# Retention and two gated layers on one core: a third raw and a third sum buffer in the rounds' dead input, weight combinations on GpSimd, 28 preparations beside the two rounds

## The chip, the core and the metric

The kernel runs on one core of one Trainium2 chip. The metric is the device time of one execution in microseconds (us); three executions of the kernel before gave 852.07, 852.21 and 853.77 us, and their median, 852.21 us, is the time before. A separately profiled execution supplies the trace; it took 853.28 us, of which the profile's span covers 851.6 us.

Engine names as in the profile: PE is TensorE (PEld its weight load), DVE is VectorE, ACT is ScalarE, POOL is GpSimd, SP is SyncE, whose queue issues nearly all transfers here.

## What is computed

```python
def reference(q, k, v, moe_w_in, moe_w_out, moe2_w_in, moe2_w_out):
    # q, k, v: (4, 8, 576, 64); scores are masked and decayed per head
    scores = q @ k.T / 8 * where(i >= j, gamma[h] ** (i - j), 0)
    x = (scores @ v) as (2304, 512)
    h = x @ moe_w_in                         # (512, 2048)
    x = (h * tanh(softplus(h))) @ moe_w_out  # (2048, 512)
    h = x @ moe2_w_in
    return (h * sigmoid(1.702 * h)) @ moe2_w_out
```

All numbers are float32. The kernel splits every float32 operand of the two layers into a high part and a low part (type float32r) and multiplies three of the four products of parts, so each block product is three matmuls.

## The kernel before

**The three stretches.** `attention` computes x into the tile `X`, which holds all 2304 tokens, 4 x 128 channels deep. `first_layer` then does the first layer's tokens 0 to 767 directly: for each of 16 weight blocks and two token blocks (512 and 256 wide) a slot with `up` (line 392) and `down` (line 413). Tokens 768 to 1535 and 1536 to 2303 follow in two *rounds*, which use the seven-product form of a 2 x 2 block product (Strassen-Winograd) for the up-projection (line 1105) and plain products for the down-projection (line 1042). `second_layer` does the second layer in three rounds of 768 tokens, seven products in both halves (up at line 648, down at line 697).

**The combined weights.** Seven products need sums of weight quarters (S1 to S4). For the first layer, `combine_first` makes them while the first layer runs, one call for each of 8 weight pairs: four additions of 128x256 by DVE (line 260), the high part by ACT, the low part by DVE (line 264), then transfers to a DRAM buffer `first_stream`, from which the rounds load them back into a ring of three buffers (line 986). For the second layer, 32 *preparations* (`prepare`, lines 275 to 337) do the same into the DRAM buffer `stream`. Before, 14 of them stand beside round one, 13 beside round two and 5 in the second layer's first round (`PREPARED_IN`).

**One preparation.** It loads raw weights (`cr`, 512 KB, line 283), clamps them on DVE (L191), converts their words on ACT (`rest`, `rebase`), sets the sign bits on DVE (L131, L203), joins the words on POOL (L207, two instructions) into the sum buffer `cy`, adds four combinations on DVE (L319 three times, L320), splits into a high part (ACT) and a low part (DVE, L328), and stores 896 KB into `stream` (line 331).

**What sets the order.** The whole program is in a fixed order per engine; nothing is rescheduled. A preparation is a generator: each `yield "skip"`, `"pool"`, `"act early"` or `"vector"` gives up control until the named position of the next table entry. A round passes 8 times over the 15 entries of `R_STEPS` (seven entries are a product of 6 matmuls, four are a down piece of 12, four do nothing on PE), so the number of yields fixes how many entries apart two steps of a preparation stand. A preparation begins every 6.5 entries (`EVERY`). `UNPREPARED` keeps preparations out of the last pass of each round. In the second layer's first round an entry is one up-product of 6 matmuls.

**What a preparation shares.** `live["cr"]` and `live["cy"]` admit two raw buffers and two sum buffers at a time. The order then has to satisfy the buffer's own waits: the join of preparation j + 2 writes the sum buffer that the store of preparation j still reads. Counted in entries from the start of preparation j, its join stands at 9, its additions at 12, its store at 20; the join of preparation j + 2 stands at 13 + 9 = 22 and its additions at 25.

**What the rounds put on the same engines.** A pass copies PSUM banks to the tile `c` on ACT (`pre`), adds a second bank on DVE (`plus`, L451 `c<-p,c`), applies the activation on ACT and makes the high part `g` (ACT) and the low part (DVE, L451 `g<-c,g`). Only two banks take products in a round (`A` and `E`), so PE may not begin a product in a bank until `pre` or `plus` has read what the bank held; between the two there is a down piece or a down piece and a product.

## Time and profile before

| What | Value |
|---|---|
| Time before, median of 3 runs | 852.21 us |
| Profiled execution, its own time | 853.28 us |
| Its span | 851.6 us |
| PE busy | 810.9 us (95%) |
| DVE busy | 597.8 us (70%) |
| ACT busy | 446.3 us (52%) |
| POOL busy | 105.9 us (12%) |
| Transfers | 219.67 MB, mean 258 GB/s |
| Chain that ended last | PE 69%, DMA 16%, DVE 6%, POOL 3%, issue 2%, ACT 2% |

PE's 95% is an average. Its share has to be read by stretch, because in most of the span PE has no gap at all and the missing time lies in a few places. Beside PE's share, the chain of waits tells what the span's end hung on: a share of DMA or POOL in it means that PE had run out of work that was ready. A busy row of POOL or DVE may also contain time in which the instruction was held up by the other engine.

### The profile page before, as it was taken

The page shows a single profiled execution, that of the slowest core. Times are in us where ns is not written, and L with a number is a line of the kernel's source. Part 1 is how long each engine was busy: PE and PEld are TensorE (multiplying, and loading weights), DVE is VectorE, ACT ScalarE, POOL GpSimd, SP SyncE. Part 2 cuts the span into 40 slices and gives each one's busy share as a digit, 9 for nine tenths or more (in the row PEclk, how much of TensorE's full clock was granted, in tenths as well). Part 3 has the DMA queues.
Part 4 walks back from the last instruction along what each step waited for, and adds up shares of the span by engine and source line. Part 5 has one row for each costly group of instructions (what it writes and reads, how often), then busy time and mean ns, then how long its engine had stood idle before and what let it go on. Part 6 is the DMA issues. An engine that isn't in the chain of part 4 may idle for free.

```text
span 851.6 us, 14187 instructions
## 1 busy us (share of the span) xinstructions
PE 810.9 (95%) x5392; PEld 764.8 (90%) x5392; DVE 597.8 (70%) x1118; ACT 446.3 (52%) x861; POOL 105.9 (12%) x124
## 2 busy tenths in 40 slices
PE   8999999999969979996989998999999999999998
PEld 7898888888969869996878997899999999999998
DVE  4886999997756657565655658688755689555776
ACT  5445777766645546554554554366333465233652
POOL 3452222220112120111111001000000000000000
PEclk9999999999979999998999999999999999999999
DMA  9974679746778785678876569987887778877775
GB/s 362 422 311 140 205 238 296 260 149 222 253 241 285 240 273 168 233 234 283 277 263 241 179 213 337 356 272 269 281 284 253 245 266 269 308 230 271 251 263 174
DMA packets 86132, 219.67 MB, mean 258 GB/s; under 512 B 5808, under 2 KB 51888, under 8 KB 78768
## 3 DMA queue, kind: packets, MB, share of 16 engines
q1 hardware_dynamic: 85920, 218.56, 75.3%
q8 instruction: 43, 0.70, 0.3%
q14 instruction: 25, 0.20, 0.1%
q10 hardware_dynamic: 144, 0.20, 0.1%
HBM read 169.98 MB, written 48.76 MB: 257 GB/s over the span
## 4 chain that ended last, share of the span: by engine, by line
PE 69%; DMA 16%; DVE 6%; POOL 3%; issue 2%; ACT 2%; SPq 0%; POOLq 0%; DVEq 0%
PE p L697 21%; PE p L648 17%; DMA stream<-cy 11%; PE h L392 8%; PE acc L413 7%; PE acc L1042 7%; PE p L1105 6%; POOL cy L207 2%; DMA unit<-qkv_dram 2%; DMA cr<-w_dram 1%; DVE cy L319 1%; PE o L901 1%; DMA raws<-w_dram 1%; PE sc L839 1%; DVE g L451 1%
## 5 line engine op out<-in xcount | busy, mean ns | idle before, releaser
L648 PE MATMUL p<-xop,ring 128*128 128x384 f32 x1008 | 176.6, 335 | 5.3 <-DVE cs L451 3.5
L648 PEld LDWEIGHTS p<-xop,ring 128*128 128x128 f32 x1008 | 174.5, 188 | 6.9 <-DVE cs L451 4.5
L697 PE MATMUL p<-g,ring 128*128 128x384 f32 x1008 | 175.2, 334 | 0.0
L697 PEld LDWEIGHTS p<-g,ring 128*128 128x128 f32 x1008 | 174.8, 188 | 0.0
L1105 PE MATMUL p<-xop,ring 128*128 128x384 f32 x672 | 132.8, 342 | 24.5 <-DVE c L451 22.5
L1042 PE MATMUL acc<-g,w 128*128 128x512 f32 (+1 forms) x768 | 147.8, 342 | 2.5 <-DVE g L451 2.5
L1042 PEld LDWEIGHTS acc<-g,w 128*128 128x128 f32 x768 | 126.8, 191 | 21.4 <-DVE g L451 4.1
L1105 PEld LDWEIGHTS p<-xop,ring 128*128 128x128 f32 x672 | 116.7, 190 | 28.3 <-DVE c L451 24.8
L122 ACT ACTIVATE g<-cs 128x384 fp32r<-128x384 f32 x168 | 79.0, 517 | 60.2 <-PE p L697 60.0
L451 DVE TENSOR_TENSOR g<-cs,g 128x384 fp32r<-128x384 f32 x168 | 90.0, 554 | 26.7 <-ACT g L122 25.1
L122 ACT ACTIVATE cs<-cs 128x384 f32<-128x384 f32 x72 | 37.7, 524 | 106.1 <-DVE cs L451 106.0
L413 PE MATMUL acc<-g,w 128*128 128x512 f32 (+1 forms) x384 | 72.3, 337 | 0.0
L413 PEld LDWEIGHTS acc<-g,w 128*128 128x128 f32 x384 | 60.2, 190 | 7.6
L207 POOL TENSOR_TENSOR cy<-cr 128x256 int32<-128x256 int32 x54 | 37.7, 718 | 231.7 <-DVE cr L203 83.0
L451 DVE TENSOR_TENSOR g<-c,g 128x384 fp32r<-128x384 f32 x64 | 37.2, 581 | 29.0 <-ACT g L122 28.4
L122 ACT ACTIVATE g<-c 128x384 fp32r<-128x384 f32 (+1 forms) x96 | 50.4, 525 | 12.4 <-PE acc L413 10.0
L122 ACT ACTIVATE cy<-cy 128x896 fp32r<-128x896 f32 (+1 forms) x40 | 38.8, 969 | 30.1 <-DVE cy L320 23.7
L451 DVE TENSOR_TENSOR cs<-cs 128x384 f32<-128x384 f32 x96 | 53.1, 553 | 0.8
L319 DVE TENSOR_TENSOR cy<-cy 128x128 f32<-128x128 f32 x96 | 25.1, 289 | 40.3 <-POOL cy L207 39.2
L207 POOL TENSOR_TENSOR raw<-raw 128x512 int32<-128x512 int32 x32 | 38.0, 1188 | 101.6 <-DVE raw L203 80.3
L122 ACT ACTIVATE raw<-raw 128x512 int32<-128x512 uint32 x64 | 41.8, 677 | 14.5 <-DVE raw L191 14.4
L122 ACT ACTIVATE c<-p 128x384 f32<-128x384 f32 x64 | 30.9, 484 | 34.7 <-PE p L1105 34.3
(90 smaller groups left out, 932.1 us busy)
## 6 DMA issues: line engine op xcount, KB each, us to landing
ring<-stream SPq DMA_DIRECT2D x112, 512.0 KB, 4.6
stream<-cy SPq DMA_DIRECT2D x32, 896.0 KB, 6.6
ring<-stream SPq DMA_DIRECT2D x28, 1024.0 KB, 4.8
raw<-w_dram SPq DMA_DIRECT2D x32, 512.0 KB, 7.5
unit<-qkv_dram SPq DMA_DIRECT2D x15, 1024.0 KB, 10.7
ring<-first_stream SPq DMA_DIRECT2D x14, 1024.0 KB, 7.2
ring<-first_stream SPq DMA_DIRECT2D x28, 512.0 KB, 5.9
cr<-w_dram SPq DMA_DIRECT2D x27, 512.0 KB, 4.3
```

Source lines behind the costliest of these rows:

```text
L122: nc.scalar.activation(out=o, in_=i, func=f, scale=scale, bias=bias)
L207: nc.gpsimd.tensor_tensor(out=o, in0=upper, in1=bits, op=ALU.add)
L319: nc.vector.tensor_tensor(out=v[:, o], in0=v[:, a], in1=v[:, b], op=op)
L392: nc.tensor.matmul(h[:, :n], lhsT=W[0, m // 2][:, m % 2, a, k * P : (k + 1) * P], rhs=xs[t, k][:, b, :n], start=((k, a, b) == order[0]), s ...
L413: nc.tensor.matmul(acc[t, e][:, :n], lhsT=W[1, m // 2][:, m % 2, a, e * P : (e + 1) * P], rhs=g[:, b, :n],  start=(begins(i) and a == 0 an ...
L451: eng.tensor_tensor(out=o, in0=a, in1=b, op=op)
L648: nc.tensor.matmul(banks[p], lhsT=w[:, k, a * P : (a + 1) * P], rhs=x[:, b, k], start=(p not in SAME and k == 0 and a == 0 and b == 0), st ...
L697: nc.tensor.matmul(banks[e, p], lhsT=w[:, e, a * P : (a + 1) * P], rhs=g[:, b], start=(p != 2 and r == 0 and a == 0 and b == 0), stop=(r = ...
L839: nc.tensor.matmul(sc[j][:n, p, :n], lhsT=kt[sl, p, :], rhs=qt[sl, p, :], start=True, stop=True)
L901: nc.tensor.matmul(o[sl, p, :n], lhsT=v[:n, p * P + 64 * j : p * P + 64 * j + 64], rhs=pm[u][j][:n, p, :n], start=(c == 0 and p == 0), sto ...
L1042: nc.tensor.matmul(acc[t, e][:, :w], lhsT=W[1, m // 2][:, m % 2, a, e * P : (e + 1) * P], rhs=g[:, b, o : o + w], start=(m == 0 and a == 0 ...
L1105: nc.tensor.matmul(bank, lhsT=w[:, a, k * P : (k + 1) * P], rhs=x[:, b, k], start=(p in (1, 2, 7) and k == 0 and a == 0 and b == 0), stop= ...
```

## The change

Five things are edited.

1. **Layout of X.** `X` was `[128, 4, 2304]`; it is now `[128, 3, 4, 768]`, so that the 768 tokens of one round are one contiguous stretch of 3072 elements in each partition. `cut` gives the old views; one store of `attention` that crosses a round's border becomes two. All other uses of `X` only change their indexing.
2. **A third raw buffer and a third sum buffer.** Once a round's input has been turned into operands, its part of `X` is dead until the round's results are written. `idle(s, o, n)` gives a piece of it. Every third preparation takes its raw weights and its sums from there; the four preparations of the second layer take three raw buffers and one sum buffer from the dead part of tokens 0 to 767, and the other sums from three further tiles. The limits on `live` go from 2 to 3.
3. **Combinations on GpSimd.** The four additions of `prepare` and the four of `combine_first` go from `nc.vector` to `nc.gpsimd`; in `prepare` they follow the two joins directly.
4. **Distances.** Clamp at entry 7 (4 before), sign at 10 (8), join and additions at 11 (9 and 12), high part at 15 (14), low part at 17 (17), store at 19 (20); the sum buffer is given back at 27 (21), the raw buffer at 14 (11).
5. **Counts.** `PREPARED_IN` goes from (14, 13, 5) to (14, 14, 4), and `UNPREPARED` is dropped: the positions are passed in the last pass of a round, too.

```diff
-UNPREPARED = (*range((NR - 1) * NE, NR * NE), *range((2 * NR - 1) * NE, 2 * NR * NE))
 EVERY = 6.5
-PREPARED_IN = (14, 13, 5)
+PREPARED_IN = (14, 14, 4)
...
-    X = keep.tile([P, NK, NT], F32, name="X")
+    X = keep.tile([P, NT // (2 * TH), NK, 2 * TH], F32, name="X")
...
+    def idle(s, o, n):
+
+        return X[:, s].rearrange("p k n -> p (k n)")[:, o : o + n]
...
         for o, a, b, op in ((s1, a21, a22, ALU.add), (s3, a11, a21, ALU.subtract), (s2, s1, a11, ALU.subtract), (s4, a12, s2, ALU.subtract)):
-            nc.vector.tensor_tensor(out=o, in0=a, in1=b, op=op)
+            nc.gpsimd.tensor_tensor(out=o, in0=a, in1=b, op=op)
+        yield "pool"
         yield "act early"
...
     def prepare(j, r, part, half):
 
-        while live["cr"] == 2:
+        late_one = j - sum(PREPARED_IN[:2])
+        s = 0 if late_one >= 0 else R_ROUNDS[j >= PREPARED_IN[0]]
+        while live["cr"] == 3:
             yield "skip"
         live["cr"] += 1
-        if j == sum(PREPARED_IN[:2]):
-            raws.append(keep.tile([P, 2, 4, P], I64, tag="side", name="raws"))
-        raw = raws[0][:, j % 2] if raws else keep.tile([P, 4, P], I64, tag=f"x{2 + j % 2}", name="cr")
-        nc.sync.dma_start(out=raw, in_=w2[r, part, half])
-        yield from pause(4)
+        if late_one >= 0:
+            raw = idle(0, late_one % 3 * 2 * DM, 2 * DM)
+        elif j % 3 == 2:
+            raw = idle(s, 4 * DM, 2 * DM)
+        else:
+            raw = keep.tile([P, 2 * DM], F32, tag=f"x{2 + j % 3}", name="cr")
+        raw = raw.rearrange("p (q n) -> p q n", q=4)
+        nc.sync.dma_start(out=raw.bitcast(I32), in_=w2[r, part, half].bitcast(I32))
+        yield from pause(7)
         yield "vector"
         clamp(raw)
-        yield "skip"
         yield "act early"
         rest(raw)
         yield "act early"
         rebase(raw, nc.scalar)
-        yield from pause(2)
+        yield "skip"
         yield "vector"
         sign(raw)
         yield "pool"
-        while live["cy"] == 2:
+        while live["cy"] == 3:
             yield "pool"
...
         join(raw[:, 0:2], bits[:, a11 : a21 + 1 : a21 - a11])
         join(raw[:, 2:4], bits[:, a12 : a22 + 1 : a22 - a12])
-        yield from pause(2)
+        for o, a, b, op in (
+            (s1, a21, a22, ALU.add),
+            (s3, a11, a21, ALU.subtract),
+            (s2, s1, a11, ALU.subtract),
+            (s4, a12, s2, ALU.subtract),
+        ):
+            nc.gpsimd.tensor_tensor(out=v[:, o], in0=v[:, a], in1=v[:, b], op=op)
+        yield from pause(3)
         live["cr"] -= 1
         yield "skip"
-        yield "vector"
-        for o, a, b, op in ((s1, a21, a22, ALU.add), (s3, a11, a21, ALU.subtract), (s2, s1, a11, ALU.subtract)):
-            nc.vector.tensor_tensor(out=v[:, o], in0=v[:, a], in1=v[:, b], op=op)
-        nc.vector.tensor_tensor(out=v[:, s4], in0=v[:, a12], in1=v[:, s2], op=ALU.subtract)
-        yield from pause(2)
         yield "act early"
...
-                    if now - BOTH not in UNPREPARED:
-                        for name in ("skip", "pool", "act early", "vector"):
-                            if name != "act early" or n_e not in (6, 7):
-                                position(name, now)
+                    for name in ("skip", "pool", "act early", "vector"):
+                        if name != "act early" or n_e not in (6, 7):
+                            position(name, now)
```

PE's own instructions keep their order throughout. Where instructions move, three places show it. Names carry their number, so that one preparation can be followed: `cr` is a raw buffer, `cy` a sum buffer, `c` and `g` are the round's own tiles, `X_60` is a raw or a sum buffer in dead input.

On DVE in round one, before: the clamp of one preparation, the low part of an older one, then the four additions of the one between them (line 319, line 320) and the sign (line 131, line 203), with the round's own `c` and `g` among them.

```order
L191 TENSOR_SCALAR cr_2475<-cr_2475 128x512
L451 TENSOR_TENSOR c_2490<-p_2519,c_2490 128x384
L328 TENSOR_TENSOR cy_2442<-cy_2442 128x7x128
L319 TENSOR_TENSOR cy_2512<-cy_2512 128x128 x3
L320 TENSOR_TENSOR cy_2512<-cy_2512 128x128
L451 TENSOR_TENSOR g_2555<-c_2490,g_2555 128x384
L131 SCALAR_TENSOR_TENSOR cr_2475<-cr_2475 128x512
L203 TENSOR_SCALAR cr_2475<-cr_2475 128x512
L451 TENSOR_TENSOR c_2576<-p_2562,c_2576 128x384
```

The same place on DVE after the change (lines shifted: clamp 201, sign 141 and 213, low part 352, `c` and `g` 475).

```order
L201 TENSOR_SCALAR cr_2404<-cr_2404 128x512
L352 TENSOR_TENSOR cy_2443<-cy_2443 128x7x128
L141 SCALAR_TENSOR_TENSOR cr_2404<-cr_2404 128x512
L213 TENSOR_SCALAR cr_2404<-cr_2404 128x512
L475 TENSOR_TENSOR c_2488<-p_2516,c_2488 128x384
L201 TENSOR_SCALAR X_60<-X_60 128x512
L475 TENSOR_TENSOR g_2553<-c_2488,g_2553 128x384
L475 TENSOR_TENSOR c_2572<-p_2559,c_2572 128x384
L475 TENSOR_TENSOR g_2591<-c_2572,g_2591 128x384
L352 TENSOR_TENSOR cy_2524<-cy_2524 128x7x128
```

The additions are gone from DVE, and with them the only instructions of DVE in the rounds that come directly behind POOL; the sign now stands two rows behind its clamp.

On POOL in round one, before: nothing but pairs of joins.

```order
L207 TENSOR_TENSOR cy_2998<-cr_2894 128x2x128 x2
L207 TENSOR_TENSOR cy_3080<-cr_2967 128x2x128 x2
L207 TENSOR_TENSOR cy_3142<-cr_3041 128x2x128 x2
L207 TENSOR_TENSOR cy_3205<-cr_3108 128x2x128 x2
L207 TENSOR_TENSOR cy_3275<-cr_3170 128x2x128 x2
```

On POOL in round one, after:

```order
L217 TENSOR_TENSOR cy_3282<-cr_3166 128x2x128 x2
L342 TENSOR_TENSOR cy_3282<-cy_3282 128x128 x4
L217 TENSOR_TENSOR cy_3354<-cr_3235 128x2x128 x2
L342 TENSOR_TENSOR cy_3354<-cy_3354 128x128 x4
L217 TENSOR_TENSOR X_60<-X_60 128x2x128 x2
L342 TENSOR_TENSOR X_60<-X_60 128x128 x4
```

Each pair of joins is followed by four additions of 128x128, and every third preparation works in `X_60`.

On ACT in round one, before: the high part of a preparation (128x7x128) among the round's copies, activations and high parts, with `rest` and `rebase` (128x512) of a later one behind it.

```order
L122 ACTIVATE cy_3080<-cy_3080 128x7x128
L122 ACTIVATE c_3140<-p_3133 128x384
L122 ACTIVATE cr_3108<-cr_3108 128x512 x2
L122 ACTIVATE c_3183<-p_3133 128x384
L122 ACTIVATE c_3140<-c_3140 128x384
L122 ACTIVATE g_3198<-c_3140 128x384
```

On ACT in round one, after:

```order
L132 ACTIVATE cy_3148<-cy_3148 128x7x128
L132 ACTIVATE X_60<-X_60 128x512
L132 ACTIVATE c_3212<-p_3124 128x384
L132 ACTIVATE X_60<-X_60 128x512
L132 ACTIVATE c_3212<-c_3212 128x384
L132 ACTIVATE g_3232<-c_3212 128x384
```

The high part is now the first instruction behind POOL's additions, and `rebase` of the next preparation and the copy `c<-p` stand behind it.

## Rows read from the trace of the kernel before

**Rows 1.** Stretches: us, then busy us (instructions) per engine, PEclk, DMA share, GB/s.

```profile
78.20:186.60 108.40, 108.40 (x626) 95.88 (x625) 104.93 (x167) 80.57 (x140) 32.10 (x27) 1.00 0.73 234
197.70:491.70 294.00, 266.99 (x1478) 244.04 (x1476) 181.76 (x363) 161.79 (x293) 37.69 (x54) 0.97 0.73 244
491.70:556.60 64.90, 59.58 (x338) 58.01 (x337) 45.30 (x95) 30.80 (x60) 5.94 (x10) 1.00 0.87 307
```

**Rows 2.** PE groups, 197.7 to 491.7: busy us, mean ns | idle before, releaser.

```profile
L1105 PE MATMUL p<-xop,ring 128*128 128x384 f32 x672 | 132.8, 342 | 24.5 <-DVE c L451 22.5 <-DMA ring<-first_stream 1.1 <-ACT c L122 0.8
L1042 PE MATMUL acc<-g,w 128*128 128x512 f32 x384 | 102.8, 402 | 2.5 <-DVE g L451 2.5
```

**Rows 3.** PE group, 491.7 to 556.6, the second layer's first up-half.

```profile
L648 PE MATMUL p<-xop,ring 128*128 128x384 f32 x336 | 59.8, 336 | 5.3 <-DVE cs L451 3.5 <-ACT s L122 1.7
```

**Rows 4.** Waits of the whole span: total us, times, longest.

```profile
POOL cy L207 <- DMA stream<-cy: 85.3, 11, 10.5
DVE cy L319 <- POOL cy L207: 39.2, 20, 4.8
DVE cr L191 <- DMA cr<-w_dram: 18.2, 13, 2.2
```

**Rows 5.** Timeline of SP's queue, 222 to 252: start, us.

```profile
236.41 0.42 SPq L331 DMA_DIRECT2D stream<-cy  x1
```

**Rows 6.** Timeline of POOL, same stretch: start, us, count [idle before, releaser].

```profile
225.33 1.99 POOL L207 TENSOR_TENSOR cy<-cr 128x256 int32<-128x256 int32 x2 [6.56 <-ACT cr L122]
...
244.55 1.18 POOL L207 TENSOR_TENSOR cy<-cr 128x256 int32<-128x256 int32 x2 [9.03 <-DMA stream<-cy]
```

**Rows 7.** Timeline of DVE, same stretch.

```profile
245.76 0.82 DVE L319 TENSOR_TENSOR cy<-cy 128x128 f32<-128x128 f32 x3 [4.81 <-POOL cy L207]
```

**Rows 8.** Timeline of PE in the rounds.

```profile
247.44 2.29 PE L1105 MATMUL p<-xop,ring 128*128 128x384 f32 x6 [6.59 <-DVE c L451]
249.52 3.99 PE L1042 MATMUL acc<-g,w 128*128 128x512 f32 x12
...
254.42 2.25 PE L1042 MATMUL acc<-g,w 128*128 128x512 f32 x12
...
394.03 3.48 PE L1042 MATMUL acc<-g,w 128*128 128x512 f32 x12
...
422.78 1.30 PE L1105 MATMUL p<-xop,ring 128*128 128x384 f32 x6 [1.10 <-DMA ring<-first_stream]
```

**Rows 9.** A short stretch behind PE's longest stall, columns as in rows 1.

```profile
249.50:251.50 2.00, 2.00 (x6) 1.61 (x6) 1.81 (x5) 0.88 (x3) 0.00 (x0) 0.50 1.13 403
```

**Rows 10.** POOL groups by shape, whole span: busy us, mean ns.

```profile
L207 POOL TENSOR_TENSOR cy<-cr 128x256 int32<-128x256 int32 x54 | 37.7, 718 | 231.7 <-DVE cr L203 83.0 <-DMA stream<-cy 69.7 <-ACT c L122 32.6
```

**Rows 11.** DVE groups by shape, 78.2 to 186.6, the first layer.

```profile
L433 DVE TENSOR_TENSOR g<-c,g 128x256 fp32r<-128x256 f32 x13 | 15.6, 1198 | 0.0
...
L260 DVE TENSOR_TENSOR cy<-raw 128x256 f32<-128x256 f32 x14 | 5.2, 413 | 1.2 <-DMA first_stream<-cy 1.2
L260 DVE TENSOR_TENSOR cy<-raw,cy 128x256 f32<-128x256 f32 x7 | 3.0, 426 | 0.2
L260 DVE TENSOR_TENSOR cy<-cy,raw 128x256 f32<-128x256 f32 x7 | 2.9, 412 | 0.0
```

**Rows 12.** Timelines in the first layer: one join on POOL.

```profile
107.15 1.15 POOL L207 TENSOR_TENSOR raw<-raw 128x512 int32<-128x512 int32 x1 [2.29 <-DVE raw L203]
```

**Rows 13.** DVE's instruction beside that join.

```profile
107.32 1.26 DVE L433 TENSOR_TENSOR g<-c,g 128x256 fp32r<-128x256 f32 x1
```

**Rows 14.** DVE groups by shape, 198 to 492, the two rounds.

```profile
L319 DVE TENSOR_TENSOR cy<-cy 128x128 f32<-128x128 f32 x81 | 21.2, 289 | 39.9 <-POOL cy L207 39.0
...
L320 DVE TENSOR_TENSOR cy<-cy 128x128 f32<-128x128 f32 x27 | 7.9, 292 | 0.9
```

**Rows 15.** The 42 ring loads of the rounds.

```profile
DMA to landing us min/median/max: 2.1/6.2/9.9
```

**Rows 16.** DVE timeline in the second layer, 486 to 560.

```profile
547.54 0.56 DVE L451 TENSOR_TENSOR cs<-p,u 128x384 f32<-128x384 f32 x1 [2.13 <-DMA stream<-cy]
```

More of the change, by code (lines that the diff above doesn't have):

```diff
@@ L299, in prepare @@
         order = (UP_ORDER, DOWN_ORDER)[part]
-        if j >= sum(PREPARED_IN[:2]):
-            at = NM - 2 + (j - sum(PREPARED_IN)) % 2
-            y = place(at).tile([P, NP, 2, P], F32R, tag=f"w{at}", name="cy")
-        elif j % 2:
-            y = keep.tile([P, NP, 2, P], F32R, tag="side", name="cy")
-        else:
-            y = temp[0].tile([P, NP, 2, P], F32R, tag="cy", name="cy")
+        n = NP * 2 * P
+        if late_one == 3:
+            y = idle(0, 2 * DM, n).bitcast(F32R)
+        elif late_one in (0, 1):
+            at = NM - 2 + late_one
+            y = place(at).tile([P, n], F32R, tag=f"w{at}", name="cy")
+        elif late_one == 2 or j % 3 == 1:
+            y = keep.tile([P, n], F32R, tag="side", name="cy")
+        elif j % 3 == 0:
+            y = temp[0].tile([P, n], F32R, tag="cy", name="cy")
+        else:
+            y = idle(s, 0, n).bitcast(F32R)
+        y = y.rearrange("p (o a n) -> p o a n", a=2, n=P)
         v = y[:, :, 1].bitcast(F32)
@@ L325, in prepare @@
         act(hi, v)
-        yield from pause(3)
+        yield from pause(2)
         yield "vector"
         nc.vector.tensor_tensor(out=y[:, :, 1], in0=v, in1=hi.bitcast(F32), op=ALU.subtract)
-        yield from pause(3)
+        yield from pause(2)
         c, step = (r * NP, 1) if part == 0 else (UP_STEPS + r, NR)
@@ L335, in prepare @@
         prepared.add((r, part, half))
-        yield "skip"
+        yield from pause(8)
         live["cy"] -= 1
@@ L377, in split_x @@
         xs[t, k] = x
-        act(x[:, 0, :n], X[:, k, o : o + n])
+        act(x[:, 0, :n], cut(k, o, n))
         return lambda: nc.vector.tensor_tensor(
-            out=x[:, 1, :n], in0=X[:, k, o : o + n], in1=x[:, 0, :n].bitcast(F32), op=ALU.subtract
+            out=x[:, 1, :n], in0=cut(k, o, n), in1=x[:, 0, :n].bitcast(F32), op=ALU.subtract
         )
@@ L459, in x_parts @@
     def x_parts(s, t3_in=None):
-        t, u = two(s)
-        x11, x12, x21, x22 = X[:, 0:2, t], X[:, 0:2, u], X[:, 2:4, t], X[:, 2:4, u]
+        x11, x12, x21, x22 = (X[:, s, k : k + 2, h : h + TH] for k in (0, 2) for h in (0, TH))
         if spare:
@@ L665, in to_x @@
             def to_x(e, quarter):
-                return X[:, e + 2 * (quarter > 20), two(s)[quarter % 10 - 1]]
+                return cut(e + 2 * (quarter > 20), two(s)[quarter % 10 - 1].start, TH)
             def leave(e, quarter, queue=nc.sync):
                 k, half = e + 2 * (quarter > 20), two(s)[quarter % 10 - 1]
-                queue.dma_start(out=out[k * P : (k + 1) * P, half], in_=X[:, k, half])
+                queue.dma_start(out=out[k * P : (k + 1) * P, half], in_=cut(k, half.start, TH))
             assert len(prepared) == 4 * NR and not under_way
@@ L914, in finish @@
                 g0 = b * S + t0
-                nc.vector.tensor_tensor(
-                    out=X[:, :, g0 : g0 + n], in0=o[:, :, :n], in1=gt[:, c, :, :n], op=ALU.mult
-                )
+                part = 0
+                while part < n:
+                    w = min(n - part, 2 * TH - (g0 + part) % (2 * TH))
+                    nc.vector.tensor_tensor(
+                        out=cut(slice(None), g0 + part, w),
+                        in0=o[:, :, part : part + w],
+                        in1=gt[:, c, :, part : part + w],
+                        op=ALU.mult,
+                    )
+                    part += w
             scores(0)
```

8 lines of the change are left out of this document (6 added, 2 removed).

## The prediction, made before the changed kernel was run

> **What bounds the kernel now.** I read the stretches first [rows 1]. From 78 to 187 us, in the first layer, PE is busy for 108.40 of 108.40 us: nothing can be won there. From 557 us to the end the second layer runs at PE's pace; the change doesn't touch it. Between the two lie the rounds (294.0 us, PE busy 267.0) and the second layer's first up-half (64.9 us, PE busy 59.6). That is where PE lacks work.
>
> Next, who is late there. In the rounds PE stood idle 24.5 us ahead of products and 2.5 us ahead of down pieces [rows 2], 27.0 us in all, of which 25.0 us ended with DVE. In the up-half it is 5.3 us [rows 3]. DVE is not short of time, though: it is busy 181.8 of 294.0 us. It stands in its own queue. The table of waits gives the order of blame [rows 4]: POOL's join waited 85.3 us for the store of a sum buffer (`stream<-cy`), DVE's additions waited 39.2 us for POOL, and DVE's clamp 18.2 us for raw weights.
>
> One stall shows the chain. The store of a sum buffer is issued at 236.41 [rows 5]. The join that writes this buffer again can begin only at 244.55, after 9.03 us of idle time put down to that store [rows 6]. DVE, in order, stands 4.81 us at its additions until 245.76 [rows 7]; the round's own `plus` is behind them, and PE gets its bank 6.59 us late, at 247.44 [rows 8]. The stall has a sequel: in the 2 us from 249.50 PE's granted clock is 0.50 [rows 9], the lower of its two levels (1.2 of 2.4 GHz), and a down piece takes 3.99 us where one at full clock takes 2.25 [rows 8].
>
> **The change, part by part.** My sums are made against the profiled execution's own 853.28 us, which is 1.07 us above the median of 852.21; I take the 1.07 off at the end. An entry of the rounds' table is 1.1 us: 294.0 - 27.0 - 3.0 = 264 us of unhindered work over 16 passes of 15 entries.
>
> *Third sum buffer.* Before, a store stood at entry 20 and the next join of its buffer at 22, two entries or 2.2 us later; the store in rows 5 and 6 needed 8. After, the join of preparation j + 3 stands at 19.5 + 11 = 30.5 and the store at 19: 11.5 entries, 12.7 us, which is more than the longest such wait (10.5 us [rows 4]). So POOL no longer waits for a store. **Third raw buffer and the distances.** The clamp now stands 7 entries (7.7 us) behind its load's issue instead of 4 (4.4 us); its longest wait was 2.2 us, so the wait goes too. On SP's queue the next load of a raw buffer stands at entry 19.5, well past the join at 11, so the ring loads queued behind it no longer stand behind a join.
>
> *Additions to POOL.* DVE loses its only wait on POOL, and 21.2 + 7.9 = 29.1 us of work in the rounds [rows 14]. The ends for one POOL addition of 128 columns: half of an undisturbed 256-wide join, 1.18 / 2 / 2 = 0.30 us [rows 6], and all of a mean join, 0.718 us [rows 10]. I take half of the mean, 0.36, because time on POOL should follow the columns. A preparation then keeps POOL for 2 x 0.718 + 4 x 0.36 = 2.9 us; ends 1.18 + 1.2 = 2.4 and 1.99 + 2.87 = 4.9.
>
> What this removes:
> - PE's idle time in the rounds: 27.0 us [rows 2]. What is late next is priced below.
> - The low clock behind the two longest stalls: 3.99 - 2.25 = 1.7 and 3.48 - 2.25 = 1.2, together 3.0 us [rows 8].
> - The up-half's 5.3 us [rows 3]. Its third gap came from a `cs` tile that had to wait 2.13 us for the last store of a preparation [rows 16]; the four that are left begin at entries 0 to 19.5, and the two sum buffers that share a tile with `cs` are stored by entry 26, where the tiles are wanted at 42 and 49.
>
> Together 35.3 us: the floor is 853.28 - 35.3 - 1.07 = 816.9 us.
>
> What it gives back:
> - *First layer.* Seven calls of `combine_first` lie in the stretch where DVE is busy 104.93 of 108.40 us [rows 1]. They free DVE of 5.2 + 3.0 + 2.9 = 11.1 us [rows 11] and load POOL with 28 additions of 256 columns at 0.59 to 0.718. If DVE is held for all of that, 28 x 0.718 = 20.1 us, DVE falls behind by 20.1 - 11.1 = 9.0, less its 3.5 us of idle time: 5.5 us by the stretch's end. If it isn't held, DVE gains and PE, full already, doesn't. Cover: `g` has three buffers, so a low part has up to three slots of 108.4 / 26 = 4.2 us before its use. Ends 0 and 5.5; I take 1.5, for the start of round one.
> - *Rounds.* ACT's high part is now the instruction that stands behind POOL. Between the join's position (11) and it (15) lie 4 entries, 4.4 us. 2.9 us fits; 4.9 would be 0.5 late, 28 x 0.5 = 14 us if PE felt all of it. Behind it on ACT stand the copies `c<-p`, for which PE waits, with a down piece (2.25 us [rows 8]) of leeway. The 28th preparation is in the load: DVE 181.8 - 29.1 = 152.7 and POOL 28 x 2.9 = 81, in all 234 us of 264 even if the two never overlapped. Ends 0 and 14; I take 3.
> - *Transfers.* The same bytes and one more preparation in 264 us raise the share from 0.73 to some 0.83, still below the up-half's 0.87 [rows 1]. Of the rounds' 42 ring loads the slowest took 9.9 us [rows 15], and one made PE wait, 1.10 us [rows 8]. Ends 0 and 15 (below); I take 2.
> - *Up-half.* One preparation fewer, denser than before: 0 to 3, I take 1.
>
> The sum: 853.28 - 35.3 + 1.5 + 3 + 2 + 1 - 1.07 = **824.4 us**. The one more store that the layout of `X` costs `attention`, and the positions now passed in a round's last pass, I cost at nothing: the first is one DVE instruction, the second lets stores leave earlier.
>
> **A rule against it.** A join on POOL runs from 107.15 for 1.15 us [rows 12]; a 256-wide DVE instruction that began at 107.32 took 1.26 us [rows 13], where DVE's 256-wide additions take 0.41 to 0.43, and all 13 of its kind average 1.198 [rows 11]. DVE seems to stand until POOL is done. The Trainium skill, page "SBUF — State Buffer", section "SBUF: two separate sides", says that GpSimd and a DVE instruction with two SBUF inputs take a shared port pair as an exclusive lock, for the whole instruction. By that, the trace agrees, and moving an addition to POOL doesn't free DVE of it. The page "GPSIMD Engine Reference", section "4.1 Engine selection", gives elementwise additions to VectorE and calls GpSimd about twice as slow; by that a 128-wide addition would take 0.58, a preparation 3.8 us of POOL, estimated, and the sum above would stay.
>
> **The rivals.**
> *Slower: the two engines hold each other up.* If all six POOL instructions of a preparation took what a disturbed join did, 1.99 / 2 = 1.0 us [rows 6], and DVE stood still meanwhile, the rounds would need 152.7 + 28 x 6.0 = 320 us, 26 more than now, and the kernel some 878 us. It decides from (294 - 152.7) / 28 = 5.05 us of POOL per preparation. For it: rows 12 and 13. Against: the undisturbed pair takes 1.18, the additions have half the columns, and `plus` reads PSUM with one operand.
> *POOL late for ACT.* 4.9 us per preparation, 14 us given back in the rounds instead of 3: 824.4 + 11 = 835. For it: four dependent instructions in a row; against: their size.
> *The ring takes over.* If all 14 of the rounds' 1 MB ring loads were as late as the one at 422.78, 14 x 1.10 = 15 us instead of 2: 824.4 + 13 = 837. For it: the raised share; against: 41 of 42 loads were in time.
> *It doesn't do what it says.* Some other release of the new buffers (dead input read late by a round's operands, `live` holding) leaves the chain as it is: 852. Against: 12.7 us between store and join.
>
> **How the numbers follow.** Forecast (817 to 832) 0.66, POOL late 0.15, the ring 0.07, no effect 0.04, slower 0.08. Faster by over 0.2%, about what a measurement of this kernel can tell from no change, is 0.66 + 0.15 + 0.07 = 0.88; within it 0.04; slower 0.08. The range runs from the floor, 816.5, to 840, past the two middle rivals; it leaves out about 0.15.
>
> **What would show it.** Right: in the rounds POOL's joins no longer wait for `stream<-cy` but for the sign; PE's idle ahead of `p` is under 6 us, no granted clock of 0.5, and the rounds last 265 to 275 us, the up-half 58 to 61. Wrong in the lock: DVE's instructions beside POOL's additions lengthen from 0.55 to 1 us and PE waits for DVE `c`. Wrong in the window: ACT's 128x896 high part shows idle time put down to POOL, and PE waits for ACT `c`. Wrong in the first layer: gaps of PE before 198 us. The forecast falls if the additions on POOL take over 0.6 us each.

## The result, and the profile after

| | Median us | All runs, us | Ratio to before [95%] |
|---|---|---|---|
| Before | 852.99 | 852.07 to 853.9 | |
| Changed | 831.41 | 830.51 to 833.2 | 0.975 [0.9728, 0.9771] |

The changed kernel is 21.6 us faster than the kernel before in the same comparison. The forecast was 824.4 us with a range of 816.5 to 840; the sign came out as forecast and the time lies in the range, 7.0 us above the forecast. The profiled execution of the changed kernel took 833.2 us.

The stretches of the kernel after answer to [rows 1]: the first layer, the two rounds with the first 2.2 us of the up-half, and the rest of the second layer's first up-half with 1.5 us of what follows it. Columns: us, then busy us (instructions) of PE, PEld, DVE, ACT and POOL, granted clock, DMA share, GB/s.

```profile
78.20:186.60 108.40, 107.23 (x612) 94.17 (x611) 107.53 (x134) 77.82 (x137) 60.87 (x54) 1.00 0.67 222
199.20:476.00 276.80, 266.19 (x1490) 243.73 (x1489) 168.21 (x261) 163.64 (x301) 110.56 (x168) 0.99 0.77 264
476.00:538.00 62.00, 58.44 (x334) 57.51 (x333) 40.93 (x74) 28.91 (x56) 13.28 (x24) 1.00 0.87 313
```

From the first product of the rounds to the first of the second layer it is now 274.7 us (199.16 to 473.84) where it was 294.0, and the up-half takes 62.7 us (473.84 to 536.53) where it took 64.9. The gain is in the rounds. POOL works 110.56 us there where it worked 37.69. In the first layer PE, which had no gap before, lacks 1.17 us of 108.40.

PE's groups of the rounds, which answer to [rows 2] (busy us, mean ns | idle before, releasers):

```profile
L1135 PE MATMUL p<-xop,ring 128*128 128x384 f32 x672 | 131.3, 340 | 9.3 <-ACT c L132 4.0 <-DVE c L475 3.9 <-DMA ring<-first_stream 1.5
L1072 PE MATMUL acc<-g,w 128*128 128x512 f32 x384 | 100.7, 397 | 1.3 <-DVE g L475 1.3
```

10.6 us of the 27.0 are left. Before, 25.0 of them ended with DVE; now ACT's copy `c<-p` ends as many as DVE's `plus` does. The table of waits says what ACT waits for (total us, times, longest), and that the join no longer waits for a store as in [rows 4]; POOL's largest waits are now for DVE's sign:

```profile
POOL cy L217 <- DVE cr L213: 70.6, 16, 20.0
...
ACT cy L132 <- POOL cy L342: 27.6, 20, 3.4
...
ACT cy L132 <- POOL cy L270: 18.7, 7, 3.2
...
ACT X L132 <- POOL X L342: 12.6, 7, 3.4
```

One stall shows the new chain. The timeline in order of time (start, us, instruction, count, idle before it and its releaser):

```profile
254.26 0.95 ACT L132 ACTIVATE X<-X 128x896 fp32r<-128x896 f32 x1 [3.04 <-POOL X L342]
...
255.12 0.66 ACT L132 ACTIVATE cr<-cr 128x512 f32<-128x512 f32 x1
...
255.81 0.69 DVE L141 SCALAR_TENSOR_TENSOR cr<-cr 128x512 int32<-128x512 int32 x1 [3.63 <-ACT cr L132]
...
257.10 2.23 POOL L217 TENSOR_TENSOR cy<-cr 128x256 int32<-128x256 int32 x2 [2.87 <-DVE cr L213]
...
259.40 2.02 POOL L342 TENSOR_TENSOR cy<-cy 128x128 f32<-128x128 f32 x4
...
261.45 0.95 ACT L132 ACTIVATE cy<-cy 128x896 fp32r<-128x896 f32 x1 [3.39 <-POOL cy L342]
...
264.38 0.47 ACT L132 ACTIVATE c<-p 128x384 f32<-128x384 f32 x1
...
264.90 1.33 PE L1135 MATMUL p<-xop,ring 128*128 128x384 f32 x6 [1.08 <-ACT c L132]
...
267.10 3.19 PE L1072 MATMUL acc<-g,w 128*128 128x512 f32 x9 [0.63 <-DVE g L475]
```

The chain feeds itself. The high part of one preparation (254.26) stood 3.04 us behind POOL; in ACT's fixed order the `rebase` of the next preparation (255.12) is behind it, and DVE's sign (255.81) stood 3.63 us for that `rebase`. So the joins of the next preparation begin late, at 257.10; with the additions they keep POOL until 261.4. ACT reaches the next high part at 258.06, only 0.96 us behind the start of these joins, and stands 3.39 us there. Round two has the same again: 3.03 us at 388.22, a sign that waits 3.60 us at 389.75, 3.39 us at 395.40. Behind the high part at 261.45, ACT's copy `c<-p` comes out at 264.38, and PE begins its product 1.08 us late. The down piece behind it runs at the lower clock, as the sequel in [rows 9] did: in this stretch the granted clock is 0.53 (columns as above).

```profile
267.10:270.70 3.60, 3.60 (x12) 3.12 (x13) 1.59 (x3) 2.01 (x4) 3.35 (x6) 0.53 1.03 335
```

POOL's groups (busy us, mean ns), and one line's shortest, median and longest duration in ns:

```profile
L342 POOL TENSOR_TENSOR cy<-cy 128x128 f32<-128x128 f32 x88 | 52.3, 604 | 5.2
...
L217 POOL TENSOR_TENSOR cy<-cr 128x256 int32<-128x256 int32 x38 | 29.3, 791 | 77.8 <-DVE cr L213 70.6 <-ACT g L132 3.8 <-issue 3.4
...
L270 POOL TENSOR_TENSOR cy<-raw 128x256 f32<-128x256 f32 x16 | 18.3, 1167 | 0.7 <-ACT w L132 0.7
```
```profile
L342 POOL TENSOR_TENSOR cy<-cy x88: 452/466/1208, 215.3 to 506.0; 128x128 f32<-128x128 f32 x88
```

An addition of 128 columns takes 0.604 us in the mean and never less than 0.452. A preparation so keeps POOL for 2 x 0.791 + 4 x 0.604 = 4.0 us in the mean.

### The profile page after: what moved, and what is told of

Read it like the earlier page. It is cut to its first block, busy times and chain, and to the rows that moved or that the text cites. A ratio compares the mean times of both kernels' runs of the same rounds, so it can differ in the third digit from the quotient of the medians.

```text
span 831.5 us, 14152 instructions
## 1 busy us (share of the span) xinstructions
PE 808.3 (97%) x5392; PEld 762.5 (92%) x5392; DVE 582.3 (70%) x959; ACT 444.2 (53%) x861; POOL 220.3 (26%) x284
## 4 chain that ended last, share of the span: by engine, by line
PE 50%; POOL 7%; ACT 5%; DVE 5%; DMA 3%; issue 1%; SPq 0%; POOLq 0%; DVEq 0%
PE p L720 21%; PE p L671 18%; PE acc L1072 6%; PE p L1135 5%; POOL cy L342 3%; POOL cy L217 2%; ACT X L132 2%; DMA ring<-first_stream 2%; POOL X L342 2%; ACT cy L132 1%; DMA ring<-stream 1%; ACT cr L132 1%; POOL X L217 1%; DVE cr L141 1%; DVE cy L352 1%
## 5 line engine op out<-in xcount | busy, mean ns | idle before, releaser
L1135 PE MATMUL p<-xop,ring 128*128 128x384 f32 x672 | 131.3, 340 | 9.3 <-ACT c L132 4.0
L475 DVE TENSOR_TENSOR g<-c,g 128x384 fp32r<-128x384 f32 x64 | 39.5, 617 | 52.2 <-ACT g L132 52.1
L132 ACT ACTIVATE cy<-cy 128x896 fp32r<-128x896 f32 (+1 forms) x30 | 29.5, 982 | 46.5 <-POOL cy L342 27.6
L342 POOL TENSOR_TENSOR cy<-cy 128x128 f32<-128x128 f32 x88 | 52.3, 604 | 5.2
L217 POOL TENSOR_TENSOR cy<-cr 128x256 int32<-128x256 int32 x38 | 29.3, 791 | 77.8 <-DVE cr L213 70.6
L416 PE MATMUL h<-x,w 128*128 128x512 f32 x192 | 46.6, 392 | 0.9 <-ACT c L132 0.9
```

The lines of the kernel that those rows point to most:

```text
L132: nc.scalar.activation(out=o, in_=i, func=f, scale=scale, bias=bias)
L217: nc.gpsimd.tensor_tensor(out=o, in0=upper, in1=bits, op=ALU.add)
L342: nc.gpsimd.tensor_tensor(out=v[:, o], in0=v[:, a], in1=v[:, b], op=op)
L416: nc.tensor.matmul(h[:, :n], lhsT=W[0, m // 2][:, m % 2, a, k * P : (k + 1) * P], rhs=xs[t, k][:, b, :n], start=((k, a, b) == order[0]), s ...
L475: eng.tensor_tensor(out=o, in0=a, in1=b, op=op)
L1135: nc.tensor.matmul(bank, lhsT=w[:, a, k * P : (k + 1) * P], rhs=x[:, b, k], start=(p in (1, 2, 7) and k == 0 and a == 0 and b == 0), stop= ...
```

## The experiments

**Theory.** Two things happen at once. The third sum buffer takes away POOL's wait for the store and with it PE's stalls; the additions on POOL take a part of that back, because ACT's high part is placed before POOL is done (the *window*). **Rivals.** The gain is that of the additions, which free DVE of 29 us and of its wait. Or the additions cost because POOL holds DVE up (the *lock*), so that a later place of the high part doesn't help. Or the distances bring the gain, and the buffers are only their condition.

Ratios below are to the kernel before, run on the same chip beside the kernel named.

**1. The changed kernel again** (`changed_again`, no edit).

> The changed kernel once more, as the measure on the same chip for the runs beside it. Expected 831 us (830.5 to 833.2 so far).

830.05 us, ratio 0.9744 [0.9718, 0.9769]. The result repeats, the wait of ACT for the additions too (28.1 us for `cy`, 13.4 us for `X`).

**2. The preparations' additions back on DVE** (`adds_on_dve`), at entry 13, the rest as changed.

```diff
+        yield from pause(2)
+        yield "vector"
...
-            nc.gpsimd.tensor_tensor(out=v[:, o], in0=v[:, a], in1=v[:, b], op=op)
-        yield from pause(3)
+            nc.vector.tensor_tensor(out=v[:, o], in0=v[:, a], in1=v[:, b], op=op)
+        yield "skip"
```

> The changed kernel with the four additions of a preparation back on VectorE, at entry 13, between the joins (11) and the high part (15); third buffers, counts, and combine_first on GpSimd stay. Theory 'buffers': the gain is the wait of POOL's join for a store, which stays away; DVE then stands at most for the two joins (1.2 to 2.2 us), and ACT's high part waits less, so the time is 826 to 836 us, within 5 us of the changed kernel. Rival 'engine': the gain is that DVE no longer stands behind POOL; then PE waits for DVE c again as before and the time is 842 us or more.

816.18 us, ratio 0.958 [0.9547, 0.9612]: 13.9 us faster than the changed kernel (experiment 1), and below the 826 to 836 us that I expected. The rival 'engine' (842 us or more) falls. DVE does take on additions and a wait for POOL again; PE's products in the rounds hardly feel it:

```profile
L1137 PE MATMUL p<-xop,ring 128*128 128x384 f32 x672 | 129.0, 337 | 2.0 <-DMA ring<-first_stream 1.2 <-ACT c L132 0.8
```
```profile
L344 DVE TENSOR_TENSOR cy<-cy 128x128 f32<-128x128 f32 x76 | 20.4, 290 | 12.5 <-POOL cy L217 11.2
```

DVE waits 11.2 us for POOL at those additions where [rows 14] has 39.0: what is left, 1.1 us at most, is about a join's own time, not the store's. The additions' move is no source of the gain; it took 13.9 us of it.

**3. The kernel before with its additions on GpSimd, two buffers** (`two_buffers_adds_on_pool`).

```diff
+        for o, a, b, op in ((s1, a21, a22, ALU.add), (s3, a11, a21, ALU.subtract), (s2, s1, a11, ALU.subtract)):
+            nc.gpsimd.tensor_tensor(out=v[:, o], in0=v[:, a], in1=v[:, b], op=op)
+        nc.gpsimd.tensor_tensor(out=v[:, s4], in0=v[:, a12], in1=v[:, s2], op=ALU.subtract)
         yield from pause(2)
         live["cr"] -= 1
-        yield "skip"
-        yield "vector"
...
-        yield from pause(2)
+        yield from pause(3)
         yield "act early"
```

> The kernel before with one thing changed: the four additions of a preparation go to GpSimd, directly behind the joins (entry 9); two raw and two sum buffers, all other distances as before. Theory 'buffers': POOL's join still waits some 5 us per preparation for a store, now ACT's high part stands behind it instead of DVE's additions, and with it the copies that PE waits for: 846 to 860 us, no clear gain. Rival 'engine': with DVE free of POOL most of the gain is there: 830 to 840 us.

853.11 us, ratio 1.0017 [0.9993, 1.0042]: no gain, as the theory had it. The wait for the store stays on POOL, and most of it now reaches PE by way of ACT instead of DVE:

```profile
ACT cy L122 <- POOL cy L316: 59.6, 24, 5.3
POOL cy L207 <- DMA stream<-cy: 51.9, 10, 7.3
...
PE p L1103 <- ACT c L122: 17.4, 7, 4.3
```

**4. The first layer's additions back on DVE** (`first_on_dve`).

```diff
-            nc.gpsimd.tensor_tensor(out=o, in0=a, in1=b, op=op)
-        yield "pool"
+            nc.vector.tensor_tensor(out=o, in0=a, in1=b, op=op)
```

> The changed kernel with combine_first's additions back on VectorE. PE's first round product began 1.4 us later in the changed kernel's trace (199.2 instead of 197.7), with 1.2 us of idle time behind ACT in the first layer. If POOL's 256-wide additions (mean 1.17 and 0.85 to 1.19 us) are the cause, the first layer has no gap again and the time is 1 to 1.5 us below the changed kernel's on this chip; if the layout of X or the attention's split store is the cause, it is the same within 0.5 us.

827.58 us, ratio 0.9714 [0.9689, 0.974]: 2.5 us faster than the changed kernel beside it, where I expected 1 to 1.5. In the changed kernel these two gaps of PE stand in the first layer; here there are none:

```profile
156.76 3.02 PE L416 MATMUL h<-x,w 128*128 128x512 f32 x12 [0.90 <-ACT c L132]
169.82 1.70 PE L416 MATMUL h<-side,w 128*128 128x256 f32 x12 [0.27 <-ACT c L132]
```

The gaps are 1.2 of the 2.5 us; the rest was not followed. What POOL's additions do to DVE in the first layer can be read from the signs of the first layer's own weights, in the changed kernel and here (78.2 to 186.6 us):

```profile
L141 DVE SCALAR_TENSOR_TENSOR raw<-raw 128x512 int32<-128x512 int32 x25 | 21.6, 865 | 0.0
```
```profile
L141 DVE SCALAR_TENSOR_TENSOR raw<-raw 128x512 int32<-128x512 int32 x26 | 17.7, 681 | 0.0
```

The same instruction takes 865 ns beside the additions on POOL and 681 without. DVE gave up 28 additions (11.1 us, [rows 11]) and is busier than before all the same: 107.53 of 108.40 us, against 104.93.

**5. All additions on DVE** (`all_on_dve`): the edits of 2 and 4 together.

> The changed kernel with all combinations back on VectorE, those of the preparations (at entry 13) and those of combine_first; third buffers, distances, counts and layout stay. adds_on_dve won 13.9 us over the changed kernel and first_on_dve 2.5 us. If the two are separate costs of the move to GpSimd, both fall away: some 35 + 2.5 = 37.5 us under the kernel before, 813 to 815 us. If the first layer's lag is hidden once the rounds run freely, it is no better than adds_on_dve, 816 us.

813.46 us, ratio 0.954 [0.9514, 0.9566], as expected. The two edits add up as nearly as these runs can tell: by the ratios 0.9744 - 0.954 of 852 us, 17 us, against 13.9 + 2.5. PE's groups in the rounds:

```profile
L1136 PE MATMUL p<-xop,ring 128*128 128x384 f32 x672 | 128.7, 337 | 0.8 <-DMA ring<-first_stream 0.8
L1073 PE MATMUL acc<-g,w 128*128 128x512 f32 x384 | 99.2, 394 | 0.0
```

The rounds last 258.8 us here, with these 0.8 us of idle time, so 258.0 us is their unhindered length, as far as these runs show it. This kernel is the base of the next ones.

**6. Window or lock: the high part two entries later** (`high_later`). All additions stay on GpSimd; the high part goes to entry 17, the low part to 19, the store to 21.

```diff
             nc.gpsimd.tensor_tensor(out=v[:, o], in0=v[:, a], in1=v[:, b], op=op)
...
-        yield "skip"
+        yield from pause(3)
```

> The changed kernel, all additions on GpSimd, with the high part two entries later (17 instead of 15) and low part and store with it (19, 21). Theory 'window': what the move costs is ACT standing at the high part until POOL is done (41 us in the trace of the changed kernel); two entries more, 2.1 us, cover most of the longest wait of 3.4 us: 817 to 823 us. Rival 'port': what it costs is that DVE and POOL hold each other up, wherever the high part stands: 828 us or more.

813.1 us, ratio 0.9536 [0.9503, 0.9568], more than I expected. Two entries bring back what experiment 5 brought, with every addition still on POOL. The additions didn't get faster, nor did they free DVE. The first row below is POOL's, the second DVE's low part of `g` in the rounds:

```profile
L342 POOL TENSOR_TENSOR cy<-cy 128x128 f32<-128x128 f32 x88 | 53.3, 616 | 5.2
```
```profile
L475 DVE TENSOR_TENSOR g<-c,g 128x384 fp32r<-128x384 f32 x64 | 40.9, 640 | 40.1 <-ACT g L132 39.9
```

With the additions on DVE that `g` took 567 ns (experiment 2), in the changed kernel 617, here 640: DVE is held up most here, and still PE is at work in 258.70 of the rounds' 259.50 us.

```profile
196.00:455.50 259.50, 258.70 (x1478) 240.74 (x1477) 176.45 (x263) 162.25 (x296) 119.81 (x168) 1.00 0.82 284
```

What a preparation looks like on POOL and ACT: the additions of one `cy` end at 253.81, and its high part comes at 257.00 with no wait ahead of it. The `rebase` of the next preparation now stands ahead of this high part, at 254.99.

```profile
250.73 3.08 POOL L342 TENSOR_TENSOR cy<-cy 128x128 f32<-128x128 f32 x4
...
254.99 0.67 ACT L132 ACTIVATE cr<-cr 128x512 f32<-128x512 f32 x1
...
257.00 0.94 ACT L132 ACTIVATE cy<-cy 128x896 fp32r<-128x896 f32 x1
```

So the place of the high part decides: two entries later nothing is lost, and DVE's longer instructions alone cost PE nothing in the rounds. The two entries do two things, though: they give POOL more time, and they take the next `rebase` out from behind the high part, which cuts the chain that fed itself. No run parts the two. That the lock also lengthens POOL's additions (0.452 us at least, 0.604 in the mean), and so filled the shorter window, is not excluded.

**7 to 11. Which of the buffers and distances bring the gain.** All additions on DVE. The edits are of one pattern, shown here in part: two buffers instead of three,

```diff
-        while live["cy"] == 3:
+        while live["cy"] == 2:
...
-        while live["cr"] == 3:
+        while live["cr"] == 2:
...
-            raw = keep.tile([P, 2 * DM], F32, tag=f"x{2 + j % 3}", name="cr")
+            raw = keep.tile([P, 2 * DM], F32, tag=f"x{2 + j % 2}", name="cr")
```

and, for the old distances, the old numbers of entries (clamp and sign shown; additions, high part, low part and store likewise):

```diff
-        yield from pause(7)
+        yield from pause(4)
         yield "vector"
         clamp(raw)
+        yield "skip"
         yield "act early"
...
-        yield "skip"
+        yield from pause(2)
         yield "vector"
         sign(raw)
```

Medians in us, with the ratio to before:

| | Two sum buffers | Three sum buffers |
|---|---|---|
| Old distances, two raw buffers | 851.85, 1.0001 [0.998, 1.0023] | 813.84, 0.955 [0.9524, 0.9577] |
| New distances, two raw buffers | 832.11, 0.9767 [0.9731, 0.9803] | 824.74, 0.9674 [0.9649, 0.9699] |
| New distances, three raw buffers | 812.59, 0.9532 [0.9508, 0.9556] | 813.46, 0.954 [0.9514, 0.9566] |

*Two sum buffers* (`two_sums_on_dve`).

> all_on_dve with two sum buffers instead of three for the preparations beside the rounds; the store stands at entry 19 and the next join of its buffer at 24, five entries (5.3 us) later, where the kernel before has two. Theory 'sum buffer': a store of 896 KB needs 4.6 to 8 us to land, so POOL and DVE behind it stand up to 3 us in some preparations: 818 to 832 us. Rival 'distance': the longer distance alone is enough: 813 to 816 us, as all_on_dve.

812.59 us: the rival. POOL still waits for stores here, 21.4 us in four waits, and it costs nothing.

*Two raw buffers* (`two_raws_on_dve`), the raw buffer given back at entry 13.

> all_on_dve with two raw buffers instead of three beside the rounds; the raw buffer is given back at entry 13, two entries behind the join, and three sum buffers stay. The load of preparation j + 2 then stands at 13 on SP's queue, with ring loads behind it, and waits for the join at 11. If the third raw buffer carries part of the gain, 818 us or more; if the join is done by then, within 1.5 us of all_on_dve.

824.74 us: the third raw buffer carries a part.

*Two and two, old distances* (`old_distances_two_and_two`): only the layout of `X`, the counts and the buffers of the last four preparations are left of the change.

> What the change leaves when buffers, distances and engine are undone: two raw and two sum buffers beside the rounds, all steps of a preparation at the entries of the kernel before, all combinations on VectorE; only the layout of X, the counts 14, 14, 4 with positions in the last passes, and the buffers of the four late preparations stay. If those carry nothing of the gain: 849 to 853 us. If one preparation fewer in the second layer is worth the shorter up-half seen after the change: 3 us less, 847 to 849 us.

*Two and two, new distances* (`two_and_two`).

> The same with the new distances (clamp at 7, join 11, additions 13, high part 15, store 19, sum buffer back at 20), still two raw and two sum buffers, all on VectorE. two_sums_on_dve showed that the third sum buffer adds nothing beside a third raw buffer; if that holds with two raw buffers, this is two_raws_on_dve again, 823 to 828 us, and the distance from store to join (5 entries instead of 2) is the main cure. If the sum buffer was only hidden by the third raw buffer: 832 us or more.

*Old distances, a third sum buffer alone* (`old_distances_three_sums`).

> old_distances_two_and_two with a third sum buffer alone. The prediction's first step said that POOL's wait for a store is cured by the third buffer (store at 20, next join of the buffer at 28.5, 8.5 entries later). If that step is right, POOL's joins no longer wait for a store and most of the stalls go: 823 to 832 us; what stays is the wait for raw weights (clamp at 4) and SP's queue behind the joins. If the third sum buffer does nothing: 848 us or more.

The first cell is the kernel before in its time and in its waits; layout, counts and the buffers of the last four preparations bring nothing, and the 3 us for one preparation fewer do not show. The rows are its wait for the store and its PE group from 199 to 474 us (642 of the rounds' 672 matmuls), which has the idle time of [rows 2] again:

```profile
POOL cy L217 <- DMA stream<-cy: 88.1, 11, 10.1
```
```profile
L1133 PE MATMUL p<-xop,ring 128*128 128x384 f32 x642 | 128.3, 345 | 25.2 <-DVE c L473 24.5 <-ACT c L132 0.8
```

One step to the right from there, a third sum buffer alone brings 38.0 us: more than the whole change. I had expected 823 to 832 us, since I held the distances for a part of the gain. The PE group in that kernel, same stretch:

```profile
L1135 PE MATMUL p<-xop,ring 128*128 128x384 f32 x660 | 126.5, 337 | 0.7 <-DVE c L475 0.7
```

One step down instead, the new distances alone bring 19.7 us. They put 5 entries between a store (19) and the next join of its buffer (13 + 11 = 24) where 2 were; the wait shrinks, but does not go, and a wait for the ring comes in its place:

```profile
POOL cy L217 <- DMA stream<-cy: 20.5, 3, 9.9
...
PE p L1132 <- DMA ring<-first_stream: 7.4, 4, 3.2
```

I had expected 823 to 828 us there; 832.11 is the rival's figure, so with two raw buffers a third sum buffer still brings some 7 us, which a third raw buffer hid. The cause of the ring's wait can be followed in `two_raws_on_dve`, which lost 11.3 us against three raw buffers. SP's queue and POOL, and the product that waited:

```profile
386.56 1.40 POOL L217 TENSOR_TENSOR X<-cr 128x256 int32<-128x256 int32 x2 [11.30 <-DVE cr L213]
387.92 1.59 POOL L217 TENSOR_TENSOR cy<-cr 128x256 int32<-128x256 int32 x2
387.99 1.89 SPq L297 DMA_DIRECT2D cr<-w_dram  x2
389.93 2.26 SPq L1015 DMA_DIRECT2D ring<-first_stream  x2
...
399.39 0.94 PE L1134 MATMUL p<-xop,ring 128*128 128x384 f32 x4 [3.36 <-DMA ring<-first_stream]
```

A raw load writes the buffer that a join reads. At the new distances a raw buffer is taken for 11 of the 13 entries that two of them allow, and the load stands two entries behind the join. When a join is late, the load stands on SP's queue until the join is done (387.92 + 1.59 = 389.51; the second load belongs to it), and the ring load behind it leaves only at 389.93. It lands 9.3 us later, and PE's product at 399.39 has waited 3.36 us for it. With old distances the join stands at 9, and the load has four entries. It still waits there, but less long; the rows are SP's raw loads behind DVE's sign in the rounds, new distances, then old ones with three sum buffers:

```profile
SPq L297 <- DVE cr L213: 49.4, 18, 6.4
```
```profile
SPq L297 <- DVE cr L213: 24.7, 18, 3.0
```

In the second kernel no product of the rounds waited for the ring.

So the third raw buffer is needed only because the distances moved the join, and with it the third sum buffer brings nothing more (812.59 and 813.46, intervals that overlap). There are two ways out of the old wait: a third sum buffer at the old distances, or the longer distances together with a third raw buffer. Each does nearly all of it, and they don't add up. The longer distances without the raw buffer do half.

**12. The best of both** (`high_later_first_on_dve`): the edits of 6 and 4.

> The candidate for the best: the changed kernel with the high part two entries later (high_later, 813.1 us) and combine_first's additions back on VectorE (worth 2.5 us in first_on_dve). If both add up: 810.5 to 812 us. If PE is at its own pace in the rounds either way and the first layer's lag is absorbed there: 813 us.

810.84 us, ratio 0.9522 [0.9497, 0.9547]: the lowest median of this study, 41 us below the kernel before and, by the ratios, about 19 below the changed one. It lies where the two edits would add up, but its interval overlaps that of experiment 6, so that they do is not shown. PE has no gap in the first layer, and none ahead of products in the rounds (199 to 474 us):

```profile
78.20:186.60 108.40, 108.40 (x625) 95.89 (x624) 104.98 (x167) 80.69 (x140) 31.93 (x27) 1.00 0.72 235
```
```profile
L1134 PE MATMUL p<-xop,ring 128*128 128x384 f32 x666 | 127.2, 337 | 0.0
```

Whether the preparations' additions are then better on POOL or on DVE these runs don't tell: 0.9522 here and 0.954 in experiment 5 have intervals that overlap.

## Why the prediction was right, and where its sizes were off

**Right: the first step.** POOL's wait for the store of a sum buffer was the start of the chain, a third buffer ends it, and PE's idle time in the rounds goes with it. The profile after has no such wait, and the third buffer alone gives 813.84 us. The sign of the forecast rested on this step and held.

**Mis-sized: ACT behind POOL, 3 us forecast, 13.9 measured.** This is the term that was furthest off. I took 0.36 us for a POOL addition, half of a join because it has half the columns. It takes 0.604 us. That is beyond the 0.6 us from which I had said that the forecast falls, and inside my ends of 0.30 and 0.718. A preparation takes 4.0 us of POOL instead of 2.9. But 4.0 still fits into the window of 4.4, so by my own sum the price alone would have changed nothing. The step that failed is the start of the window: I had put it at the join's entry, 4.4 us ahead of the high part, as if the join were never late. The join waits for DVE's sign, the sign for ACT's `rebase`, and `rebase` stands behind the high part of the preparation before; one late high part makes the next join late, and at 261.45 the window was 0.96 us. So the high part waited 27 times, 40.2 us in all. In the rounds PE felt 4.0 + 3.9 + 1.3 = 9.2 us as idle time behind ACT's and DVE's results, and 4.1 us as slower matmuls ([rows 2] and the groups after against 128.7 and 99.2 us in experiment 5: 131.3 - 128.7 and 100.7 - 99.2). Together 13.3; experiment 2 measures 13.9. The rival "POOL late for ACT" (835 us, 0.15) named this mechanism, and its 14 us is the measured size, but by luck: it came from 4.9 us of POOL in each preparation, with a window that starts on time, where the runs show 4.0 us and a late start.

The sentence that I took from the Trainium skill, page "GPSIMD Engine Reference", section "4.1 Engine selection", that a two-input addition is about twice as slow on GpSimd, was the better price: 0.604 against 0.290 us on DVE (experiment 2) is a factor of 2.1, so the trace agrees with it. In the first layer, with 1.167 us against 0.413 [rows 11], the factor is 2.8.

**Mis-sized: the low clock, 3.0 us forecast, 9.0 measured.** I counted the two longest down pieces. All of the rounds' matmuls ran at 342 and 402 ns in [rows 2] and run at 337 and 394 without stalls (experiment 5): 132.8 - 128.7 = 4.1 and 102.8 - 99.2 = 3.6 us. With the smaller groups PE was busy for 267.0 us of the rounds [rows 1], at a granted clock of 0.97, and is for 258.0 without stalls, at 1.00. So the unhindered rounds are 258, not 264 us, and the floor was 6 us too high: 810.9 instead of 816.9 (the range put it at 816.5). The best kernel runs at 810.84. The two errors partly cancel: 11 us given back too little, 6 us removed too little. That the time still lies in the likeliest case, 817 to 832, is luck.

**Nearly right: the first layer, 1.5 us forecast, 2.5 measured** (experiment 4). The 256-wide additions took 1.17 us on POOL where I had 0.59 to 0.718 and DVE needs 0.41. DVE's `combine_first` time was freed, but its other instructions beside POOL's grew by more than that (experiment 4), and the high part of each combination now waits for POOL (18.7 us), with ACT's copies for the first layer behind it.

**Right: the transfers, 2 us forecast, 1.5 measured.** Two ring loads made PE wait in the rounds; the share rose to 0.77 only, and to 0.82 in the kernel without stalls (experiment 6). **Mis-sized: the up-half.** 58 to 61 us forecast, 62.7 measured. It is 61.8 in the same kernel again (experiment 1), 59.7 in experiment 6, and with all additions on DVE 60.9 (experiment 5) and 62.6 (old distances, three sum buffers). So a share of POOL's lateness in it, for which I had 1 us, is not shown.

**What I had said would show it.** The joins wait for the sign and the rounds take 274.7 us (265 to 275 forecast): as said. PE's idle ahead of `p` under 6 us and no clock near 0.5: wrong, 9.3 us and 0.53. The signs that I had named for the window (idle time of ACT's 128x896 high part put down to POOL, PE waiting for ACT's `c`) are what the profile shows, and the sign for the first layer, too.

**Fell: the lock.** DVE's instructions beside POOL's additions do lengthen, `g<-c,g` from 567 to 617 and 640 ns. The Trainium skill, page "SBUF — State Buffer", section "SBUF: two separate sides", has GpSimd and a two-input DVE instruction exclude each other; by that, the trace agrees in kind. It costs nothing in the rounds: the kernel in which DVE is held up most (experiment 6) has 0.8 us of gaps in them. DVE has time to spare there, 176.45 of 259.50 us busy. In the first layer it has none (107.53 of 108.40), and there the lock may carry a part of the 2.5 us; no run parts it from ACT's wait. **Fell: the ring, and no effect.** The ring did take over in one place, but only with two raw buffers at the new distances.

**What the sum couldn't show.** The change bundles two cures of the same wait (a sum buffer and distances), a condition of the second (a raw buffer), and a move that costs (the additions). I priced the bundle as if its parts added up. They don't: the sum buffer alone gives 38.0 us, the distances alone 19.7, both with the raw buffer 38 to 39.

What stays open: the late sign is explained from these two stalls, and no run parts the time of the window from the order of `rebase` and high part; and the 40.2 us of ACT's waits were not followed one by one to PE.

## What to carry to other kernels

When an instruction waits for the transfer that empties its buffer, count the distance between the two in units of the schedule, and put that beside the transfer's time: one more buffer was enough here, and a few entries more were, too, once the buffer that they kept longer got a third copy; without it they gave half. Look at what the longer distance holds on to, and at what stands behind it on the same queue. When work moves to a slower engine, see whether the consumer behind it has to move, too: here two entries of the schedule were worth some 17 us, with the slow instructions left where they were. A window between two engines holds only if both arrive at their entries on time; follow what the first one waits for. Price small instructions from a row of their own size and engine; half the columns was not half the time here.

## What the runs showed of the hardware

- A GpSimd addition of 128 columns of float32 took at least 0.452 us, in the mean 0.604 (0.616 in experiment 6), while a 256-wide join of int32 took 0.791 in the changed kernel. Half the columns cost three quarters of the time.
- A 256-wide float32 addition on GpSimd took 1.167 us in the mean of the largest group in the first layer, where DVE is busy in 107.53 of 108.40 us, against 0.413 on DVE [rows 11]. DVE's 128x512 sign took 865 ns there, against 681 without the additions on GpSimd.
- Short stalls cost more than their idle time. In the rounds before, PE's 27.0 us of idle time came with 9.0 us more of busy time for the same matmuls. In the changed kernel, behind stalls of 1.08 and 0.63 us, the granted clock was 0.53 in a stretch of 3.6 us (near the lower of its levels, 1.2 of 2.4 GHz).
